# Rotated q and k through DRAM in two transfers, and more raw weight pieces fetched at the start

## The chip, the cores and the metric

The kernel runs on one core of a Trainium2 chip. A core has five engines with a queue of instructions each, run in order: TensorE (PE in the profile; its weight loads are shown apart as PEld), VectorE (DVE), ScalarE (ACT), GpSimd (POOL) and SyncE (SP). SP computes nothing here; it starts DMA transfers. The engines wait for each other through semaphores. The metric is the time of one execution on the device in microseconds (us). The kernel before takes 928.59 us, the median of three runs.

## The reference

The first half is a gated linear recurrence with complex decays, for 4 batches x 8 heads, 768 time steps and heads of 48. The second half is a feed-forward with RMS norm and SwiGLU on the 3072 resulting rows of 384. Cut to its core:

```python
mag = np.sqrt(a_re * a_re + a_im * a_im)
scale = np.minimum(mag, 0.999) / (mag + 1e-06)
a_re_n, a_im_n = (a_re * scale, a_im * scale)
for t in range(S):
    ar, ai = (a_re_n[:, :, t, :, None], a_im_n[:, :, t, :, None])
    new_re = ar * S_re - ai * S_im
    new_im = ar * S_im + ai * S_re
    kv = np.einsum('bhd,bhe->bhde', k[:, :, t], v[:, :, t])
    S_re, S_im = (new_re + kv, new_im)
    y[:, :, t] = np.einsum('bhd,bhde->bhe', q[:, :, t], S_re)
...
rms = np.sqrt(np.mean(x * x, axis=-1, keepdims=True) + 1e-06)
xn = x / rms * rms_g
g = xn @ w_gate
silu = g * (1.0 / (1.0 + np.exp(-g)))
val = xn @ w_val
return (silu * val @ w_out).astype(np.float32)
```

The weights of the feed-forward arrive as 64-bit floats, 384 x 1536 twice and 1536 x 384 once.

## The kernel before

The time steps are cut into chunks of 128 (`C`), six to a batch, 24 in all (`N`). Two chunks are a unit (12 units), three chunks are a group (8 groups). Everything is computed in 32-bit floats.

**Gates, a unit at a time** (`gates(u)`). `load_gates(u)` (L514) fetches the decays `re`, `im` and `q`, `k` of a unit, each as a tile of 128 partitions x 3 x 256. DVE and ACT work out, along the time axis, the running product `p` of the magnitudes (a scan, L579), its last value per chunk (`ends`, L582), and the running phase. q is multiplied by the magnitude and k by its inverse. Then both are multiplied by cosine and sine of the phase (L607 to L610), which gives four tiles `k`, `ks`, `q`, `qs`. In these tiles the features lie on 128 partitions in three blocks.

**The copies.** TensorE needs them otherwise: 96 partitions (48 cosine rows, 48 sine rows), and the eight heads side by side. L619 does this by DMA from SBUF to SBUF. For each chunk and each of q and k there are two parts of three blocks, 12 transfers of 64 KB. L625 moves the decays of a chunk, six transfers of half a KB. L629 loads `v` of the chunk. All are issued by SP.

**Chunks.** `scores(n)` multiplies k and q of every head (L705), DVE masks the product (L707), and PE transposes k (L716). `finish(n)` adds the chunk to the state (L728, multiplied by the decay on DVE), makes y from the masked scores and from the state (L739, L741), norms it (L745 to L751) and transposes it to `xT` (L758, L759).

**Feed-forward, a group at a time** (`feed_forward(g)`). For each of 12 blocks of 128 columns PE makes the gate and the value (L776), ACT the SiLU (L779), DVE the product `hT`. Then PE makes the three output chunks with `wo` (L787), ACT copies them out of PSUM (L792), SP stores them (L794).

**Weights.** `load_weights` yields 18 pieces of 768 KB: six for `wg` and six for `wv` in turns, then six for `wo`. `narrow` fetches one (L656) into one of two buffers `raw` and turns it into 32-bit floats by one instruction on ACT (L662) and six on DVE (lines L663 to L671 through the helpers L501 and L504, and directly at L665 and L669). The first group's feed-forward asks for two pieces every second block and for the six of `wo` after its last block.

**Order.** The program is written as generators: `run` steps the work of chunk n, and between its steps work of the last group's feed-forward (`filler`) and of the next unit's gates (`ahead`). A planner then lays out each engine's queue when the kernel is built. It takes an instruction when it reckons its operands and buffers ready, and prefers the one written earlier, so that later work moves forward into gaps. From then on each queue's order is fixed, DMA issues among it. The lines that the change touches are those of `load_gates`, the end of `gates`, `narrow` and `load_weights`, the decay in `finish` (L730), the weight calls in `feed_forward`, and the main loop.

Of the kernel before, what the change touches and what calls it, by code (L numbers as in the profile page):

```python
# [28 lines left out]
P = 128  # L29
# [442 lines left out]
def fast(tc, ctx, qT, kT, v, a_re, a_im, w_gate, w_val, w_out, rms_g, out, H, bad):  # L472
# [23 lines left out]
    ffn = ctx.enter_context(tc.tile_pool(name="ffn", bufs=2))  # L496
# [12 lines left out]


    UN = [dict() for _ in range(NU)]

    def load_gates(u):
# [14 lines left out]

    first_loads = load_gates(0)

    zeros = consts.tile([P, T], FP32, name="zeros")
    nc.gpsimd.memset(zeros, 0.0)
# [9 lines left out]
    nc.gpsimd.memset(mid, -(RE_MAX + RE_MIN) / 2)  # L542
    width = consts.tile([P, 1], FP32, name="width")
    nc.gpsimd.memset(width, -(RE_MAX - RE_MIN) / 2)
    ends = consts.tile([P, NU, ND, UC], FP32, name="ends")
    range_ = consts.tile([P, NU], FP32, name="range_")

    def gates(u):
# [1 line left out]
        re, im, q, k = (t[x] for x in ("re", "im", "q", "k"))  # L550
        act_ = nc.scalar.activation

        s, w, y, r, p, ks, qs = (prep.tile([P, ND, T], FP32, tag=x, name=x)
                                 for x in ("s", "w", "y", "r", "p", "ks", "qs"))
        act_(out=s, in_=re, func=AF.Square)
        act_(out=w, in_=im, func=AF.Square)
        tt(s, s, w, ALU.add)
# [18 lines left out]
        wc = w.rearrange("p j (c t) -> p j c t", t=C)  # L576
# [27 lines left out]
        act_(out=s, in_=im, func=AF.Sin, scale=2 * PI)  # L604
        act_(out=y, in_=w, func=AF.Sin, scale=-2 * PI, bias=halfpi)
        yield
        tt(ks, k, s)  # L607
        tt(k, k, y)
        tt(qs, q, s)
        tt(q, q, y)  # L610
        rot = {"kc": k, "ks": ks, "qc": q, "qs": qs}
        yield
        for i in range(UC):
            n = u * UC + i
            for name in ("k", "q"):
                to = U[n][name] = unit.tile([D2, H, C], FP32, tag=name, name=name, bufs=3)
                for a, part in enumerate("cs"):
                    for j in range(ND):
                        nc.sync.dma_start(  # L619
                            out=to[a * D + j * L:a * D + (j + 1) * L],  # L620
                            in_=rot[name + part][:, j, i * C:(i + 1) * C])
            de = U[n]["decay"] = unit.tile([D2, H], FP32, tag="decay", name="decay", bufs=5)
            for a in range(2):
                for j in range(ND):
                    nc.sync.dma_start(  # L625
                        out=de[a * D + j * L:a * D + (j + 1) * L],
                        in_=ends[:, u, j, i:i + 1])
            U[n]["v"] = unit.tile([C, H, D], FP32, tag="v", name="v", bufs=3)
            nc.sync.dma_start(out=U[n]["v"].rearrange("t h d -> t (h d)"),  # L629
                              in_=v[n * C:(n + 1) * C, :])  # L630
        yield


# [13 lines left out]


    FW = 2 * P

    def narrow(stage, to, src):

        rows, cols = to.shape[1:]
        n = rows * cols
        raw = stage.tile([P, rows, 2 * cols], I32, tag="raw", name="raw", bufs=2)
        nc.sync.dma_start(out=raw, in_=src)  # L656
# [8 lines left out]
        nc.vector.tensor_scalar(out=t, in0=g, scalar1=3, scalar2=0x3FFFFFFF,  # L665
                                op0=ALU.logical_shift_left, op1=ALU.bitwise_and)
# [6 lines left out]
    def load_weights(stage):  # L673

        for f in range(0, DF, FW):
            for to, ap in ((wg, w_gate), (wv, w_val)):
                to = to[:, :, f:f + FW]
                if ap.dtype == FP32:
                    nc.sync.dma_start(out=to, in_=ap.rearrange("(c p) f -> p c f", p=P)[:, :, f:f + FW])
                else:  # L680
                    narrow(stage, to, ap.bitcast(I32).rearrange("(c p) f -> p c f", p=P)
                           [:, :, 2 * f:2 * (f + FW)])
                yield
        for c in range(0, NF, 2):
            to, ap = wo[:, c:c + 2], w_out
            if ap.dtype == FP32:
                nc.sync.dma_start(out=to, in_=ap.rearrange("(c p) f -> p c f", p=P)[:, c:c + 2])
            else:
                narrow(stage, to, ap.bitcast(I32).rearrange("(c p) f -> p c f", p=P)[:, c:c + 2])
            yield  # L690


    U = [dict() for _ in range(N)]
    G = [dict() for _ in range(NG)]

    def scores(n):
# [23 lines left out]
    def finish(n):  # L720
# [4 lines left out]
        if n % NCH < NCH - 1:  # L725
            ps = ps_a.tile([D2, H, D], FP32, tag="a", name="state_ps")
            for h in range(H):
                nc.tensor.matmul(ps[:, h], lhsT=u["kt"][:, h], rhs=vv[:, h], start=True, stop=True)  # L728
            new = unit.tile([D2, H, D], FP32, tag="state", name="state")
            decay = u["decay"].unsqueeze(2).to_broadcast([D2, H, D])  # L730
# [30 lines left out]
        yield  # L761


    def feed_forward(g, pieces):
        xT = G[g]["xT"]
        hT = ffn.tile([P, NF, GT], FP32, tag="hT", name="hT", bufs=1)
        for f in range(NF):
            fs = slice(f * P, (f + 1) * P)
            if f * P % FW == 0:
                next(pieces, None)  # L770
                next(pieces, None)
            gp = ps_g.tile([P, GT], FP32, tag="g", name="gate_ps")
            vp = ps_g.tile([P, GT], FP32, tag="g", name="val_ps")
            for p_, w_ in ((gp, wg), (vp, wv)):
                for d in range(ND):
                    nc.tensor.matmul(p_, lhsT=w_[:, d, fs], rhs=xT[:, d], start=d == 0,  # L776
                                     stop=d == ND - 1)
# [35 lines left out]
    for n in range(N + 1):  # L813
# [13 lines left out]
        if n % GC == 0 and n:  # L827
            for _ in filler:
                pass
            filler = feed_forward(n // GC - 1, pieces)  # L830

    ne = NU * ND * UC
    ok = act.tile([P, 2 * ne + NU], FP32, tag="ok", name="ok", bufs=1)
# [63 lines left out]
```

## Time and profile before

The profiled execution is a separate one; its own time stands beside the span, which runs from its first to its last instruction.

| | us |
|---|---|
| three runs | 928.59, 923.82, 930.76 |
| the profiled execution | 935.99 |
| its span | 934.3 |
| PE busy | 798.5 (85%) |
| PEld busy | 544.1 (58%) |
| DVE busy | 430.5 (46%) |
| ACT busy | 370.7 (40%) |
| POOL busy | 17.1 (2%) |
| first matmul starts at | 43.57 |

In the rows of the profile, L705 is line 705 of the kernel, and `out<-in` names tiles. "x16" is a count. In a row of the groups, the numbers behind the first bar are the busy time in all and the mean of one instruction in ns. What stands behind the second bar is idle time of that engine just before. In a timeline the first two numbers are start and duration, and a bracket at the end tells how long the engine had been idle and what released it. In a DMA row the numbers are KB of one transfer and the median time from issue to landing. In a row of waits they are the total, the count and the longest. The granted clock of TensorE is given as a share of its full speed; its mean over the execution was 0.916.

### The profile page before, as it was taken

Reading aid. Unit: us, or ns where it says so; the run is one execution under the profiler, and the core shown is the slowest. Engines: PE = TensorE matmul, PEld = TensorE weight load, DVE = VectorE, ACT = ScalarE, POOL = GpSimd, SP = SyncE. Lnnn points to the kernel's source line nnn. Section 1 sums busy time; section 2 is a strip of 40 time slices with the busy share of each in tenths; the row PEclk is TensorE's granted clock in tenths of the full one; section 3 lists DMA queues with packets and bytes.
Section 4 is the critical chain, followed back from the end, with each engine's and each line's share of the span. In section 5 each row is a group of like instructions: output and inputs, shape, how many; then the busy total and the mean of one; then the engine's idle time right before and its main releaser. Section 6 shows DMA issues by size and latency. Waiting matters only on the chain.

```text
span 934.3 us, 9261 instructions
## 1 busy us (share of the span) xinstructions
PE 798.5 (85%) x3370; PEld 544.1 (58%) x3370; DVE 430.5 (46%) x641; ACT 370.7 (40%) x530; POOL 17.1 (2%) x41
## 2 busy tenths in 40 slices
PE   0134885388688899999999999999999999999997
PEld 0133865245446557667666767676667666765554
DVE  5896454797797364362554622735612101110110
ACT  5756354552653282461657613727411111110110
POOL 0000000000000000000000000000000000000000
PEclk9998575688797999898999999999999999899999
DMA  7422333147344232232023222221211010000000
GB/s 227 104 81 69 87 93 102 40 111 201 88 118 107 76 99 58 69 93 60 21 66 94 77 59 77 60 59 24 63 26 43 8 43 1 1 1 26 1 1 29
DMA packets 105574, 62.14 MB, mean 67 GB/s; under 512 B 28720, under 2 KB 99376, under 8 KB 105520
## 3 DMA queue, kind: packets, MB, share of 16 engines
q1 hardware_dynamic: 105520, 61.46, 24.1%
q8 instruction: 29, 0.48, 0.2%
q14 instruction: 25, 0.20, 0.1%
HBM read 37.75 MB, written 4.72 MB: 45 GB/s over the span
## 4 chain that ended last, share of the span: by engine, by line
PE 76%; DVE 10%; ACT 3%; issue 2%; DMA 1%; POOL 0%; DVEq 0%; ACTq 0%; SPq 0%
PE out_ps L787 20%; PE gate_ps L776 20%; PE val_ps L776 18%; PE y_ps L739 5%; PE y_ps L741 4%; PE s_ps L705 3%; PE state_ps L728 3%; PE kt_ps L716 1%; PE xT_ps L758 1%; DVE t L504 1%; DVE g L504 1%; DVE w L504 1%; DVE im L504 1%; DVE p L579 1%; DMA raw<-in_w_gate_dram 1%
## 5 line engine op out<-in xcount | busy, mean ns | idle before, releaser
L776 PE MATMUL val_ps<-xT,wv 128*128 128x384 f32 x576 | 210.4, 503 | 24.8 <-DVE wv L501 24.2
L776 PE MATMUL gate_ps<-xT,wg 128*128 128x384 f32 x576 | 217.0, 516 | 2.3 <-DVE wg L501 1.7
L787 PE MATMUL out_ps<-wo,hT 128*128 128x384 f32 x576 | 200.9, 507 | 8.5 <-DVE wo L501 7.2
L776 PEld LDWEIGHTS val_ps<-xT,wv 128*128 128x128 f32 x576 | 113.0, 197 | 106.6 <-DVE wv L501 26.3
L787 PEld LDWEIGHTS out_ps<-wo,hT 128*128 128x128 f32 x576 | 112.4, 199 | 85.2 <-issue 9.3
L776 PEld LDWEIGHTS gate_ps<-xT,wg 128*128 128x128 f32 x576 | 112.6, 202 | 75.1 <-issue 12.3
L501 DVE TENSOR_TENSOR hT<-val_ps,sg 128x384 f32<-128x384 f32 x96 | 53.3, 555 | 219.0 <-PE val_ps L776 194.5
L779 ACT ACTIVATE sg<-gate_ps 128x384 f32<-128x384 f32 x96 | 47.1, 490 | 180.2 <-PE gate_ps L776 177.0
L705 PE MATMUL s_ps<-q,k 96*128 96x128 f32 x384 | 55.5, 305 | 56.5 <-DMA k<-k 43.6
L705 PEld LDWEIGHTS s_ps<-q,k 96*128 96x128 f32 x384 | 54.6, 220 | 62.5 <-issue 44.0
L739 PE MATMUL y_ps<-v,am 128*128 128x48 f32 x384 | 78.9, 303 | 0.0
L741 PE MATMUL y_ps<-state,q 96*128 96x48 f32 x320 | 70.5, 306 | 0.0
L739 PEld LDWEIGHTS y_ps<-v,am 128*128 128x128 f32 x384 | 65.6, 221 | 0.8
L792 ACT COPY ot<-out_ps 128x384 f32<-128x384 f32 x24 | 11.4, 477 | 118.1 <-PE out_ps L787 112.1
L741 PEld LDWEIGHTS y_ps<-state,q 96*128 96x128 f32 x320 | 57.1, 222 | 0.0
L745 ACT ACTIVATE x<-y_ps 128x384 f32<-128x384 f32 x24 | 11.8, 491 | 107.5 <-PE y_ps L741 98.6
L728 PE MATMUL state_ps<-v,kt 128*96 128x48 f32 x320 | 34.9, 269 | 22.8 <-DVE am L707 22.8
L728 PEld LDWEIGHTS state_ps<-v,kt 128*96 128x96 f32 x320 | 34.6, 187 | 27.5 <-DVE am L707 23.7
L707 DVE TENSOR_TENSOR am<-s_ps,causal 128x512 f32<-128x512 f32 x48 | 32.5, 687 | 39.2 <-PE s_ps L705 39.1
L746 DVE TENSOR_SCALAR ssq<-ssq 128x1 f32<-128x1 f32 x24 | 3.7, 153 | 71.9 <-ACT x L745 71.9
L717 ACT COPY kt<-kt_ps 128x384 f32<-128x384 f32 x40 | 17.3, 478 | 46.6 <-PE kt_ps L716 46.6
L779 ACT ACT_TABLE_LOAD x27 | 34.6, 1283 | 0.5
(97 smaller groups left out, 714.3 us busy)
## 6 DMA issues: line engine op xcount, KB each, us to landing
re<-in_a_re_dram SPq DMA_DIRECT2D x36, 128.0 KB, 2.8
im<-in_a_im_dram SPq DMA_DIRECT2D x36, 128.0 KB, 2.8
q<-in_q_dram SPq DMA_DIRECT2D x24, 192.0 KB, 3.1
k<-in_k_dram SPq DMA_DIRECT2D x24, 192.0 KB, 3.7
v<-in_v_dram SPq DMA_DIRECT2D x24, 192.0 KB, 2.8
raw<-in_w_gate_dram SPq DMA_DIRECT2D x6, 768.0 KB, 5.6
raw<-in_w_val_dram SPq DMA_DIRECT2D x6, 768.0 KB, 5.2
q<-qs SPq DMA_DIRECT2D x72, 64.0 KB, 2.4
```

Source lines behind the costliest of these rows:

```text
L501: nc.vector.tensor_tensor(out=o, in0=x, in1=y, op=op)
L504: nc.vector.scalar_tensor_tensor(out=o, in0=x, scalar=c, in1=y, op0=op0, op1=op1, **kw)
L705: nc.tensor.matmul(ps[:, h], lhsT=k[:, a * hh + h], rhs=q[:, a * hh + h], start=True, stop=True)
L707: nc.vector.tensor_tensor(out=am[:, a * hh:(a + 1) * hh], in0=ps, op=ALU.mult, in1=causal.unsqueeze(1).to_broadcast([C, hh, C]))
L717: nc.scalar.copy(out=kt[:, a * hh:(a + 1) * hh], in_=ps)
L728: nc.tensor.matmul(ps[:, h], lhsT=u["kt"][:, h], rhs=vv[:, h], start=True, stop=True)
L739: nc.tensor.matmul(ps[:, h], lhsT=am[:, h], rhs=vv[:, h], start=True, stop=prev is None)
L741: nc.tensor.matmul(ps[:, h], lhsT=q[:, h], rhs=prev[:, h], start=False, stop=True)
L745: nc.scalar.activation(out=x, in_=y, func=AF.Square, accum_out=ssq)
L776: nc.tensor.matmul(p_, lhsT=w_[:, d, fs], rhs=xT[:, d], start=d == 0, stop=d == ND - 1)
L779: nc.scalar.activation(out=sg, in_=gp, func=AF.Silu)
L787: nc.tensor.matmul(ps, lhsT=hT[:, f, i * C:(i + 1) * C], rhs=wo[:, f], start=f == 0, stop=f == NF - 1)
```

## The change

The four products of the rotation are written straight into one tile `rot` of 128 x 12 x 2 x 129, with the chunk's decay in column 129 beside both parts of q. One DMA writes a chunk's share of it to a tile in DRAM, and one reads it back in the layout that TensorE needs: 96 partitions, k and q, eight heads, 129 columns. This replaces the 18 transfers of L619 and L625. q and k as loaded have one buffer instead of two, and `v` is fetched with the gates' inputs, into four buffers instead of three.

Raw weight pieces are fetched apart from narrowing them. The first five are asked for before the first gates: three into a pool `early` of three buffers, two into the stage pool as before. From piece 3 on, piece i + 2 is asked for when piece i is to be narrowed. The first three are narrowed, in the program's order, at the end of step n = 3. The pool `early` is closed there and the feed-forward's pool opened in its place; the pieces after them are narrowed as far as a block needs. The first unit's `im` is issued on ACT's queue, and an extra activation at the start makes ACT load its function table. The loads of the second unit are written behind the first unit's gates.

```diff
+    dram = ctx.enter_context(tc.tile_pool(name="dram", bufs=2, space=DRAM))
...
+            queue = nc.scalar if u == 0 and name == "im" else nc.sync
             for j in range(ND):
-                nc.sync.dma_start(out=t[name][:, j], in_=rows[j][:, :, c * C:c * C + T])
-        for name, ap in (("q", qT), ("k", kT)):
-            t[name] = prep.tile([P, ND, T], FP32, tag=name, name=name, bufs=2)
+                queue.dma_start(out=t[name][:, j], in_=rows[j][:, :, c * C:c * C + T])
+        for name, ap in (("k", kT), ("q", qT)):
+            t[name] = prep.tile([P, ND, T], FP32, tag=name, name=name)
...
+        for n in range(u * UC, (u + 1) * UC):
+            U[n]["v"] = unit.tile([C, H, D], FP32, tag="v", name="v", bufs=4)
+            nc.sync.dma_start(out=U[n]["v"].rearrange("t h d -> t (h d)"),
+                              in_=v[n * C:(n + 1) * C, :])
...
+    rot = consts.tile([P, 4 * ND, UC, C + 1], FP32, name="rot")
+    nc.vector.memset(rot[:, :, :, C:], 0.0)
...
+    nc.scalar.activation(out=width, in_=width, func=AF.Abs_reciprocal_sqrt)
+    nc.gpsimd.memset(width, -(RE_MAX - RE_MIN) / 2)
...
+        nc.vector.tensor_copy(
+            out=rot[:, 2 * ND:, :, C].rearrange("p (a j) c -> p a j c", j=ND),
+            in_=ends[:, u].unsqueeze(1).to_broadcast([P, 2, ND, UC]))
...
-        tt(ks, k, s)
-        tt(k, k, y)
-        tt(qs, q, s)
-        tt(q, q, y)
-        rot = {"kc": k, "ks": ks, "qc": q, "qs": qs}
+        for i, (x, f) in enumerate(((k, y), (k, s), (q, y), (q, s))):
+            tt(rot[:, i * ND:(i + 1) * ND, :, 0:C], by_chunk(x), by_chunk(f))
...
-            for name in ("k", "q"):
-                to = U[n][name] = unit.tile([D2, H, C], FP32, tag=name, name=name, bufs=3)
-                for a, part in enumerate("cs"):
-                    for j in range(ND):
-                        nc.sync.dma_start(
-                            out=to[a * D + j * L:a * D + (j + 1) * L],
-                            in_=rot[name + part][:, j, i * C:(i + 1) * C])
-            de = U[n]["decay"] = unit.tile([D2, H], FP32, tag="decay", name="decay", bufs=5)
...
+            way = dram.tile([4 * DM, C + 1], FP32, tag="way", name="way")
+            nc.sync.dma_start(out=way.rearrange("(r p) t -> p r t", p=P), in_=rot[:, :, i])
+            to = unit.tile([D2, 2, H, C + 1], FP32, tag="kq", name="kq", bufs=3)
+            nc.sync.dma_start(out=to.rearrange("d x h t -> d x (h t)"),
+                              in_=way.rearrange("(x d h) t -> d x (h t)", x=2, h=H))
+            U[n]["k"], U[n]["q"] = to[:, 0, :, 0:C], to[:, 1, :, 0:C]
+            U[n]["decay"] = to[:, 1, :, C:]
...
-    def narrow(stage, to, src):
+    narrowed = [0]
+    EARLY = 3
+
+    def fetch(pool, to, src):
+        raw = pool.tile([P, to.shape[1], 2 * to.shape[2]], I32, tag="raw", name="raw")
+        nc.sync.dma_start(out=raw, in_=src)
+        return raw
+
+    def narrow(stage, to, raw):
...
+        for i in range(EARLY + 2):
+            get(i)
+        yield
+        for i, (to, ap, c, f) in enumerate(parts):
+            if i >= EARLY and i + 2 < len(parts):
+                get(i + 2)
+            if i in raws:
+                narrow(stage, to, raws.pop(i))
+            narrowed[0] += 1
+            yield
...
-                next(pieces, None)
-                next(pieces, None)
+                while narrowed[0] < 2 * (f * P // FW + 1):
+                    next(pieces)
...
-    pieces = load_weights(stage)
-    load_gates(1)
+    first = ExitStack()
+    pieces = load_weights(first.enter_context(tc.tile_pool(name="early", bufs=EARLY)), stage)
+    next(pieces)
     for _ in gates(0):
         pass
+    load_gates(1)
...
+            if n == GC:
+                for _ in range(EARLY):
+                    next(pieces)
+                first.close()
+                ffn = ctx.enter_context(tc.tile_pool(name="ffn", bufs=2))
```

The tile `ok` of the final range check now shares a buffer with `x` of the chunks.

More of the change, by code (lines that the diff above doesn't have):

```diff
@@ L511, in fast @@
     UN = [dict() for _ in range(NU)]
+    U = [dict() for _ in range(N)]
     def load_gates(u):
@@ L551, in gates @@
         act_ = nc.scalar.activation
-        s, w, y, r, p, ks, qs = (prep.tile([P, ND, T], FP32, tag=x, name=x)
-                                 for x in ("s", "w", "y", "r", "p", "ks", "qs"))
+        s, w, y, r, p = (prep.tile([P, ND, T], FP32, tag=x, name=x)
+                         for x in ("s", "w", "y", "r", "p"))
         act_(out=s, in_=re, func=AF.Square)
@@ L574, in gates @@
         stt(w, w, EPS_MAG, r, ALU.subtract, ALU.min)
[L576 removed]
+        by_chunk = lambda x: x.rearrange("p j (c t) -> p j c t", t=C)
+        wc = by_chunk(w)
         nc.vector.tensor_copy(out=starts[:, :, :, 0:1], in_=wc[:, :, :, 0:1])
@@ L614, in gates @@
             n = u * UC + i
-            for name in ("k", "q"):
-                to = U[n][name] = unit.tile([D2, H, C], FP32, tag=name, name=name, bufs=3)
-                for a, part in enumerate("cs"):
-                    for j in range(ND):
-                        nc.sync.dma_start(
-                            out=to[a * D + j * L:a * D + (j + 1) * L],
-                            in_=rot[name + part][:, j, i * C:(i + 1) * C])
-            de = U[n]["decay"] = unit.tile([D2, H], FP32, tag="decay", name="decay", bufs=5)
[L623 to L630, printed above, removed]
+            way = dram.tile([4 * DM, C + 1], FP32, tag="way", name="way")
[5 more added lines that the diff above has]
+            U[n]["decay"] = to[:, 1, :, C:]
         yield
@@ L649, in fast @@
     FW = 2 * P
-    def narrow(stage, to, src):
+    narrowed = [0]
[5 more added lines that the diff above has]
+    def narrow(stage, to, raw):
         rows, cols = to.shape[1:]
         n = rows * cols
-        raw = stage.tile([P, rows, 2 * cols], I32, tag="raw", name="raw", bufs=2)
-        nc.sync.dma_start(out=raw, in_=src)
         words = raw.rearrange("p c f -> p (c f)").rearrange("p (n two) -> p n two", two=2)
@@ L671, in narrow, with load_weights, get @@
         tt(to, as_to(t.bitcast(FP32)), to, ALU.add)
-    def load_weights(stage):
+    def load_weights(early, stage):
+        parts = []
         for f in range(0, DF, FW):
[L676 to L685, printed above, removed]
+            parts += [(to[:, :, f:f + FW], ap, slice(0, ND), f) for to, ap in ((wg, w_gate), (wv, w_val))]
+        parts += [(wo[:, c:c + 2], w_out, slice(c, c + 2), 0) for c in range(0, NF, 2)]
+        raws = {}
+        def get(i):
+            to, ap, c, f = parts[i]
             if ap.dtype == FP32:
-                nc.sync.dma_start(out=to, in_=ap.rearrange("(c p) f -> p c f", p=P)[:, c:c + 2])
+                nc.sync.dma_start(out=to, in_=ap.rearrange("(c p) f -> p c f", p=P)[:, c, f:f + to.shape[2]])
             else:
-                narrow(stage, to, ap.bitcast(I32).rearrange("(c p) f -> p c f", p=P)[:, c:c + 2])
+                raws[i] = fetch(early if i < EARLY else stage, to, ap.bitcast(I32)
+                                .rearrange("(c p) f -> p c f", p=P)[:, c, 2 * f:2 * (f + to.shape[2])])
+        for i in range(EARLY + 2):
[7 more added lines that the diff above has]
+            narrowed[0] += 1
             yield
-    U = [dict() for _ in range(N)]
     G = [dict() for _ in range(NG)]
@@ L729, in finish @@
             new = unit.tile([D2, H, D], FP32, tag="state", name="state")
-            decay = u["decay"].unsqueeze(2).to_broadcast([D2, H, D])
+            decay = u["decay"].to_broadcast([D2, H, D])
             if prev is None:
@@ L761, in finish, with feed_forward @@
         yield
-    def feed_forward(g, pieces):
+    def feed_forward(g, pieces, ffn):
         xT = G[g]["xT"]
@@ L829, in fast @@
                 pass
-            filler = feed_forward(n // GC - 1, pieces)
+            if n == GC:
[3 more added lines that the diff above has]
+                ffn = ctx.enter_context(tc.tile_pool(name="ffn", bufs=2))
+            filler = feed_forward(n // GC - 1, pieces, ffn)
     ne = NU * ND * UC
-    ok = act.tile([P, 2 * ne + NU], FP32, tag="ok", name="ok", bufs=1)
+    ok = act.tile([P, DM], FP32, tag="x", name="ok", bufs=1)[:, 0:2 * ne + NU]
     for to, in_, limit, op in ((ok[:, 0:ne], ends.rearrange("p u j c -> p (u j c)"), P_MIN, ALU.is_ge),
```

3 lines of the change are left out of this document (1 added, 2 removed).

## The prediction

> **What bounds the kernel now.** I read, in this order: the page's busy shares and slices, the stages by windows, the queue of SyncE in order of time, the waits, the groups by line, and the DMA rows. First the page: the span, and the busy share of TensorE (PE) in 40 equal slices.
>
> ```profile
> span 934.3 us, 9261 instructions
> PE   0134885388688899999999999999999999999997
> ```
>
> From the fifteenth slice on (327 us, and by the windows below from 311 us) PE is busy without a gap; before that it isn't. The windows give the stages, with VectorE (DVE) and ScalarE (ACT) beside it (columns: PE, PEld, DVE, ACT, POOL, clock, DMA share, GB/s):
>
> ```profile
> core 0: us, PE busy (x) PEld busy (x) DVE busy (x) ACT busy (x) POOL busy (x), PEclk, DMA share, GB/s
> 0.00:12.00 12.00, 0.00 (x0) 0.00 (x0) 1.77 (x2) 6.78 (x8) 2.27 (x17) 1.00 0.66 179
> 12.00:60.00 48.00, 5.04 (x24) 4.77 (x24) 44.13 (x61) 30.93 (x37) 0.00 (x0) 1.00 0.52 148
> 60.00:176.00 116.00, 75.49 (x381) 68.13 (x381) 63.64 (x92) 58.68 (x82) 2.75 (x5) 0.70 0.28 76
> 176.00:311.00 135.00, 100.67 (x382) 63.91 (x383) 114.35 (x161) 59.41 (x80) 2.45 (x3) 0.83 0.42 113
> 311.00:905.00 594.00, 594.00 (x2513) 393.89 (x2512) 206.04 (x326) 213.45 (x323) 9.61 (x16) 0.97 0.17 47
> ```
>
> So the time has two parts. From 311 us PE sets the end, at 594.00 busy of 594.00, and nothing off PE can shorten that part. Before 311 us PE waits for things that DVE makes: the gates of each pair of chunks, and the weights, which DVE narrows from 64-bit words in 18 pieces. The second part of the feed-forward of the first three chunks needs the last piece, so the ramp ends when piece 18 is narrowed. When DVE works on pieces is shown by its instructions that read a raw piece, two for each piece:
>
> ```profile
> 0.00:60.00 60.00, 5.71 (x6) 2.70 (x3) 1.00 0.55 154
> 60.00:176.00 116.00, 0.00 (x0) 0.76 (x1) 0.70 0.28 76
> 176.00:311.00 135.00, 28.57 (x30) 12.79 (x15) 0.83 0.42 113
> ```
>
> Three pieces before 60 us, none from 60 to 176 us, fifteen after. In the middle window DVE had 116 - 63.64 = 52.4 us free and used none of it for weights. The queue of SyncE (SP, which issues every DMA) says why:
>
> ```profile
> 32.11 0.54 SPq L656 DMA_DIRECT2D raw<-in_w_gate_dram  x1
> ...
> 38.96 0.96 DVE L504 SCALAR_TENSOR_TENSOR wv<-raw,g 128x768 f32<-128x768 uint32 x1
> ...
> 65.85 1.91 SPq L619 DMA_DIRECT2D k<-k  x3
> ...
> 73.58 3.80 SPq L625 DMA_DIRECT2D decay<-ends  x6
> ...
> 140.84 0.49 SPq L656 DMA_DIRECT2D raw<-in_w_val_dram  x1
> 141.37 0.49 SPq L656 DMA_DIRECT2D raw<-in_w_gate_dram  x1
> ```
>
> Piece 2 (counting from 0) is fetched at 32 us. The buffer for piece 3 is free at 38.96 + 0.96 = 39.9 us, when DVE has last read piece 1. Yet piece 3 is fetched at 140.84 us, behind the copies of rotated q and k (L619) and decays (L625) of three units. The queue runs in order, and it also stands still for the results that it copies. PE then stands for the late weights (waits of SP from 30 to 315 us, and of PE up to 315 us):
>
> ```profile
> SPq L619 <- DVE k L501: 46.9, 4, 21.3
> SPq L656 <- DVE wv L504: 33.3, 5, 16.8
> PE val_ps L776 <- DVE wv L501: 24.2, 4, 12.0
> PE out_ps L787 <- DVE wo L501: 7.2, 3, 3.3
> ```
>
> **The change, part by part.** *The copies.* Per unit of two chunks L619 and L625 issue 2 x (12 + 6) = 36 DMAs; three take 1.91 us and six 3.80 us, so 0.63 us each and 36 x 0.63 = 22.7 us of SP. Afterwards there are 2 x 2 = 4, about 2.5 us. Over 12 units SP loses some 240 us of issuing. None of it is on PE's path after 311 us. Before that it is what stands ahead of the pieces.
>
> *The pieces.* Five are fetched before the first gates instead of two, three into buffers of their own. Every later one is asked for as soon as a stage buffer is free, with 4 DMAs of rotations ahead of it per unit instead of 36. So DVE can use its free time between 60 and 176 us. How much? It won't reach 100%, since it waits in order for PE and ACT. The rate with pieces at hand is in the windows: 44.13/48 = 92% from 12 to 60 us, 114.35/135 = 85% from 176 to 311 us. I take 85%, the window with the same mixture of feed-forward and gates. From 60 to 176 us DVE then does 0.85 x 116 = 98.6 us, 35.0 us more than now. That is seven pieces at the price of one:
>
> ```profile
> L504 DVE SCALAR_TENSOR_TENSOR g<-wg,raw 128x768 f32<-128x768 f32 x6 | 5.7, 949 | 0.0
> L504 DVE SCALAR_TENSOR_TENSOR t<-g,t 128x768 int32<-128x768 int32 x18 | 17.1, 952 | 0.2
> L665 DVE TENSOR_SCALAR t<-g 128x768 int32<-128x768 int32 x18 | 9.9, 551 | 0.1
> ```
>
> The third form comes twice in a piece (L665, L669) and the first two stand for four passes: 4 x 0.95 + 2 x 0.55 = 4.9 us. What is left for the last window is 114.35 - 35.0 = 79.4 us, at 85% 93.7 us: the ramp ends at 176 + 93.7 = 269.7 instead of 311 us, **-41 us**. PE has room for this: it was busy for 181 us up to 311 us, at a low clock, some 141 us at full clock (5 + 75.49 x 0.70 + 100.67 x 0.83), and from 44 to 270 us there are 226. Ends: nothing gained (0), and DVE full from 60 us on, where the idle 52.4 + (135 - 114.35) = 73 us all go (-73).
>
> *The way through DRAM.* Rotated q, k and decays of a chunk are written (4 x 384 rows of 516 bytes, 792 KB) and read back, and the read waits on SP for the write. The nearest rows:
>
> ```profile
> k<-in_k_dram SPq DMA_DIRECT2D x24, 192.0 KB, 3.7
> raw<-in_w_gate_dram SPq DMA_DIRECT2D x6, 768.0 KB, 5.6
> k<-ks SPq DMA_DIRECT2D x72, 64.0 KB, 2.5
> out_dram<-ot SPq DMA_DIRECT2D x24, 192.0 KB, 1.9
> 34.06 0.95 DVE L501 TENSOR_TENSOR k<-k,y 128x768 f32<-128x768 f32 x1
> 43.57 3.76 PE L705 MATMUL s_ps<-q,k 96*128 96x128 f32 x16 [43.57 <-DMA k<-k]
> 60.76 0.68 DVE L707 TENSOR_TENSOR am<-s_ps,causal 128x512 f32<-128x512 f32 x1
> 62.83 0.94 DVE L501 TENSOR_TENSOR k<-k,r 128x768 f32<-128x768 f32 x1
> ```
>
> The read has long rows: 5.6 us as a raw piece of the same size. The write has short rows: between 5.6 us and four of the 512-byte loads one after another, 4.1 x 3.7 = 15.2 us; I take 7 us, nearer to the raw piece, as a store of 192 KB lands in 1.9 us. The first chunk's way is then 12.6 us against 43.57 - 35.01 = 8.6 now: **+4 us** in unit 0. It may be less, since DVE reaches the scores late: it masks the first at 60.76 us though PE had them at 47.3 us, a cover of 13 us. As DVE's order is made anew I don't count on that cover for unit 0, but do for the later ones, where the ramp has other work; without it the price is 4 us a unit, with some five units in the ramp. While SP stands for a write, the raw fetches and loads behind it wait up to 7 us, twice a unit, which two raw buffers cover.
>
> The Trainium skill says, in "DMA: Bandwidth & Descriptors", section "Issuing engines are not separate DMA queues", that the time to start a DMA is usually small beside the DMA itself. By that rule fewer DMAs would be worth next to nothing and the sum would be the second rival's. The trace has 0.63 us of issue beside a landing of 2.5 us for the small copies, but 36 issues in a row, so the rule does not hold for a queue that runs in order.
>
> *The start.* im goes out on ACT's queue and the table of functions is loaded before the data come.
>
> ```profile
> 4.94 1.28 ACT L555 ACT_TABLE_LOAD   x1 [4.94 <-DMA re<-in_a_re_dram]
> 7.28 0.84 ACT L556 ACTIVATE w<-im 128x768 f32<-128x768 f32 x1 [0.20 <-DMA im<-in_a_im_dram]
> 8.14 1.28 ACT L558 ACT_TABLE_LOAD   x1
> ```
>
> One load of 1.28 us, perhaps both, leaves ACT's path: **-2 us** (0 to -2.6).
>
> *The rest, at nothing.* The new copy of the decays into rot is one small DVE instruction a unit: under 0.55 us, the shortest pass above, so under 3 us in the ramp and 0 after it. k and q in one buffer each: the next unit's loads wait for the rotations, done at 35 us for unit 0, while unit 1's k is first scaled at 62.83 us; a load of 3.7 us fits, and would cost 3.7 us a unit if not. The feed-forward's buffers take the memory of the three early pieces; DVE has read those before 60 us already now, and hT is first written when three chunks are through. PE reads k and q from rows of 516 bytes. No row shows such a pitch; the nearest are two forms that read am and q in blocks of 512 bytes:
>
> ```profile
> L739 PE MATMUL y_ps<-v,am 128*128 128x48 f32 x384 | 78.9, 303 | 0.0
> L741 PE MATMUL y_ps<-state,q 96*128 96x48 f32 x320 | 70.5, 306 | 0.0
> ```
>
> They differ by 3 ns with 128 and 96 rows, which says little of an odd pitch. I take zero; 384 + 160 + 320 = 864 matmuls read k or q, and 45 ns on each would eat the whole gain.
>
> *Sum.* -41 + 4 - 2 = -39 us. The profiled run took 935.99 us, 1.7 us beyond its span, and so would give 897. It lies 7.4 us above the median of 928.59, from which the same difference gives **890 us**.
>
> **The rivals.** *Second: DVE's free time can't be filled.* The waits of DVE from 44 to 315 us speak for it:
>
> ```profile
> DVE ssq L746 <- ACT x L745: 27.6, 8, 6.4
> DVE xT L759 <- PE xT_ps L758: 13.7, 6, 4.6
> DVE hT L501 <- PE val_ps L776: 10.7, 4, 4.4
> ```
>
> Together 52.0 us, in which DVE stands at the head of its order for PE and could not narrow anything, unless pieces are placed ahead of the waiting instruction. If pieces only move and the waits stay, the gain is the start and at most two pieces (2 x 4.9 us) less the 4 us: 0 to -8 us, 920 to 929. Against it: with pieces at hand DVE ran at 92% and 85%.
>
> *Third, slower: the round trip paces the chunks.* If the write takes 15.2 us, the second chunk of a unit arrives 2 x 15.2 + 5.6 = 36 us after the rotation, against 8.6 + 12 x 0.63 = 16.2 now. That is 20 us more; less the cover of 13 us it is 7 us a unit, 35 us over the five or so units of the ramp, and SP stands meanwhile, so the pieces gain nothing: about 964 us. It decides from a round trip of 8.6 + 13 = 21.6 us. Against it: a store of 192 KB lands in 1.9 us, sooner than loads of that size.
>
> *Fourth: more than forecast.* With the pieces ahead, DVE needs fewer gates done before the ramp ends, and PE's clock (0.70 and 0.83 in the ramp) rises as its gaps close: up to the end of -73 us, some 855.
>
> **How the numbers follow.** The forecast (gain 15 to 60 us, 868 to 914) gets 0.68, the fourth 0.12, the second 0.12, the third 0.08. About 1% (9 us) is what a measurement can tell here. Faster by more is the forecast with the fourth, 0.80; within is the second, 0.12; slower 0.08. The range reaches from the end at -75 us, 853, to within the second rival, 925.
>
> **What would show it.** Right: pieces read by DVE between 60 and 176 us (some 14 raw-reading instructions there, now 0); DVE at about 85% in that window; PE without gaps from about 270 us; the waits of PE for wv and wo together under 10 us; SP with 4 long DMAs a unit, the write landing in about 7 us. Wrong: PE waiting for the read of k and q again and again in the ramp; DVE's idle time under ssq, xT and hT as long as now; s_ps, kt_ps or y_ps matmuls longer in the stage after the ramp; a raw fetch again 50 us or more after its buffer came free.

## The result, and the profile after

| | before | changed |
|---|---|---|
| median of 4 runs, us | 929.61 | 888.31 |
| range, us | 923.82 to 930.76 | 884.13 to 890.75 |
| the profiled execution, us | 935.99 | 884.13 |
| its span, us | 934.3 | 882.3 |
| PE busy in it, us | 798.5 | 773.3 |
| span less PE busy, us | 135.8 | 109.0 |

The changed kernel takes 0.9563 of the time before, 95% interval 0.9507 to 0.9619, a gain of 40.6 us; 890 was predicted. The two profiled spans differ by 52.0 us, but the profiled execution of before lies 6.4 us above its median and that of the changed kernel 4.2 us below, which is 10.6 of these. Among the kernels below, some executions are slower than the others of the same kernel; the ratios leave these out, the medians do not, and the profiles of `early_only` and `way_twice` show such executions, so sizes read from these two are only rough.

The page of the changed kernel first: span, PE's total, and PE's slices.

```profile
span 882.3 us, 8797 instructions
PE 773.3 (88%) x3370; PEld 530.1 (60%) x3370; DVE 426.8 (48%) x654; ACT 356.2 (40%) x520; POOL 23.2 (3%) x42
PE   0051879888879999999999999999999999999997
```

PE is full from the thirteenth slice on, not the fifteenth. Then its windows, with the same columns as before, and the instructions of DVE that read a raw piece (DVE, ACT, clock, DMA share, GB/s):

```profile
60.00:176.00 116.00, 80.53 (x406) 65.06 (x404) 92.29 (x138) 68.14 (x92) 6.13 (x5) 0.74 0.64 154
60.00:271.00 211.00, 156.90 (x719) 118.56 (x718) 167.18 (x247) 111.41 (x152) 8.61 (x8) 0.77 0.58 146
271.00:882.30 611.30, 605.18 (x2587) 400.35 (x2586) 214.69 (x345) 206.32 (x322) 12.20 (x16) 0.99 0.26 63
```

```profile
60.00:176.00 116.00, 12.61 (x14) 4.54 (x5) 0.74 0.64 154
176.00:311.00 135.00, 16.83 (x18) 7.29 (x8) 0.87 0.50 130
```

Fourteen raw-reading instructions stand where there were none. The last piece is narrowed at 271 us, and PE's last gap of the ramp ends half a microsecond before (DVE, then PE, in order of time):

```profile
270.14 0.94 DVE L501 TENSOR_TENSOR wo<-t,wo 128x768 f32<-128x768 f32 x1
```

```profile
270.56 0.55 PE L774 MATMUL xT_ps<-ident,xn 128*128 128x128 f32 x3 [1.46 <-ACT xn L767]
```

What is left at 271 us is what was left before at 311 us. The same window of the kernel before is

```profile
311.00:934.30 623.30, 617.30 (x2584) 407.29 (x2582) 206.60 (x327) 214.89 (x326) 9.61 (x16) 0.97 0.17 46
```

2584 matmuls there, 2587 here. So 40 us of the difference between the spans are the ramp. Of these, 26.9 us are idle time of PE (129.8 us up to 311 us before, 102.9 us up to 271 us now), and 13.1 us are its busy time (181.2 and 168.1 us, for 787 and 785 matmuls). The mean granted clock of the two stretches is 0.81 and 0.82, so the clock's mean does not account for the 13.1 us; where they come from stays open. The other 12 us lie in the stage without gaps, at a clock of 0.97 against 0.99, and 10.6 us is how far the two executions lie from their medians. The waits of PE up to 315 us, those of before that the prediction did not show and then those of after:

```profile
PE s_ps L705 <- DMA k<-k: 43.6, 1, 43.6
PE state_ps L728 <- DVE am L707: 22.8, 4, 12.5
PE xT_ps L758 <- ACT xn L751: 15.0, 6, 3.4
PE s_ps L705 <- DVE am L707: 12.9, 1, 12.9
```

```profile
PE s_ps L721 <- DMA kq<-way: 77.3, 5, 48.8
PE xT_ps L774 <- ACT xn L767: 15.4, 6, 6.4
PE gate_ps L792 <- DVE wg L501: 4.8, 2, 3.1
```

The waits for `wv` and `wo` (31.4 us) and for the mask `am` (35.7 us) are gone. In their place PE waits for k and q from DRAM, 48.8 us for the first chunk (43.6 before) and 77.3 - 48.8 = 28.5 us in four later units.

### The profile page after: what moved, and what is told of

Same layout as the page of the kernel before. It is cut to its first block, busy times and chain, and to the rows that moved or that the text cites. A ratio compares the mean times of both kernels' runs of the same rounds, so it can differ in the third digit from the quotient of the medians.

```text
span 882.3 us, 8797 instructions
## 1 busy us (share of the span) xinstructions
PE 773.3 (88%) x3370; PEld 530.1 (60%) x3370; DVE 426.8 (48%) x654; ACT 356.2 (40%) x520; POOL 23.2 (3%) x42
## 4 chain that ended last, share of the span: by engine, by line
PE 80%; DMA 10%; DVE 6%; ACT 2%; issue 1%; SPq 1%; POOL 0%; ACTq 0%; DVEq 0%
PE val_ps L792 20%; PE gate_ps L792 20%; PE out_ps L803 19%; PE s_ps L721 6%; PE y_ps L755 5%; DMA way<-rot 4%; PE y_ps L757 4%; DMA kq<-way 4%; PE state_ps L744 3%; PE kt_ps L732 2%; DVE rot L501 1%; PE xT_ps L774 1%; DMA raw<-in_w_gate_dram 1%; DVE p L592 1%; DVE g L504 1%
## 5 line engine op out<-in xcount | busy, mean ns | idle before, releaser
L792 PE MATMUL gate_ps<-xT,wg 128*128 128x384 f32 x576 | 209.4, 501 | 5.5 <-DVE wg L501 4.8
L803 PE MATMUL out_ps<-wo,hT 128*128 128x384 f32 x576 | 192.8, 491 | 0.2
L792 PEld LDWEIGHTS gate_ps<-xT,wg 128*128 128x128 f32 x576 | 109.0, 196 | 73.7 <-issue 7.9
L803 PEld LDWEIGHTS out_ps<-wo,hT 128*128 128x128 f32 x576 | 108.7, 192 | 71.7 <-issue 1.8
L721 PE MATMUL s_ps<-kq 96*128 96x128 f32 x384 | 57.2, 311 | 77.3 <-DMA kq<-way 77.3
L721 PEld LDWEIGHTS s_ps<-kq 96*128 96x128 f32 x384 | 55.5, 224 | 84.0 <-DMA kq<-way 55.6
L755 PE MATMUL y_ps<-v,am 128*128 128x48 f32 x384 | 76.0, 294 | 0.0
L757 PE MATMUL y_ps<-state,kq 96*128 96x48 f32 x320 | 68.2, 298 | 0.0
L757 PEld LDWEIGHTS y_ps<-state,kq 96*128 96x128 f32 x320 | 55.1, 215 | 0.3
L765 POOL TENSOR_TENSOR rs<-ssq,mhalf 128x1 f32<-128x1 f32 x24 | 20.8, 867 | 754.7 <-DVE ssq L762 754.7
```

The source lines that it names most:

```text
L721: nc.tensor.matmul(ps[:, h], lhsT=k[:, a * hh + h], rhs=q[:, a * hh + h], start=True, stop=True)
L755: nc.tensor.matmul(ps[:, h], lhsT=am[:, h], rhs=vv[:, h], start=True, stop=prev is None)
L757: nc.tensor.matmul(ps[:, h], lhsT=q[:, h], rhs=prev[:, h], start=False, stop=True)
L765: nc.gpsimd.tensor_tensor(out=rs, in0=ssq, in1=mhalf, op=ALU.pow)
L803: nc.tensor.matmul(ps, lhsT=hT[:, f, i * C:(i + 1) * C], rhs=wo[:, f], start=f == 0, stop=f == NF - 1)
```

## The experiments

Each edit makes the planner lay all queues out anew, so one kernel's times say less than the agreement of several. The table gives the ratio to the kernel before with its 95% interval, the gain (one less the ratio, times 929.6 us), and from each profile PE's idle time (span less PE busy), the raw-reading instructions of DVE from 60 to 176 us, and the start of the first scores. Idle time and start are left empty for `early_only` and `way_twice`.

| kernel | ratio | gain, us | PE idle, us | raw 60-176 | first scores, us |
|---|---|---|---|---|---|
| changed | 0.9563 (0.9507 to 0.9619) | 40.6 | 109.0 | 14 | 48.79 |
| way_only | 0.9725 (0.9659 to 0.9791) | 25.6 | 120.2 | 12 | 53.22 |
| early_only | 1.008 (0.9988 to 1.0172) | -7.4 | | 3 | |
| raw_on_pool | 0.9552 (0.9506 to 0.9597) | 41.6 | 116.7 | 20 | 49.75 |
| raw_on_act | 0.9544 (0.9470 to 0.9618) | 42.4 | 115.0 | 21 | 54.05 |
| early_pool | 0.9652 (0.9596 to 0.9708) | 32.4 | 117.9 | 22 | 45.2 |
| no_start | 0.9612 (0.9559 to 0.9664) | 36.1 | 117.5 | 11 | 52.68 |
| early0 | 0.9584 (0.9526 to 0.9642) | 38.7 | 112.9 | 13 | 50.42 |
| way_twice | 0.9786 (0.9723 to 0.9849) | 19.9 | | 8 | |
| way_halves | 0.9489 (0.9433 to 0.9544) | 47.5 | 100.5 | 12 | 46.63 |
| later_on_pool | 0.9894 (0.9848 to 0.9940) | 9.9 | 138.1 | 10 | 51.05 |
| pool_start | 0.9497 (0.9440 to 0.9554) | 46.8 | 110.8 | 20 | 43.67 |
| pool_start2 | 0.9599 (0.9537 to 0.9662) | 37.3 | 113.4 | 20 | 42.6 |

**Do the pieces stand behind SP's copies?** The theory of the prediction against one in which DVE cannot use its free time. `way_only` is the kernel before with the copies through DRAM (and q and k as loaded in one buffer each) and nothing else of the change:

```diff
-            for name in ("k", "q"):
...
+            nc.sync.dma_start(out=way.rearrange("(r p) t -> p r t", p=P), in_=rot[:, :, i])
+            to = unit.tile([D2, 2, H, C + 1], FP32, tag="kq", name="kq", bufs=3)
+            nc.sync.dma_start(out=to.rearrange("d x h t -> d x (h t)"),
+                              in_=way.rearrange("(x d h) t -> d x (h t)", x=2, h=H))
```

> The kernel before with one part of the change: rotated q, k and decays go through DRAM in one write and one read a chunk (q and k as loaded in one buffer each); weight pieces, v and the start stay as before. Queue theory (the 36 small copies of a unit in SP's queue hold back the weight pieces, and taking them out is the gain): at least 30 of the 41 us gained, 885 to 900 us, ten or more raw-reading instructions on DVE between 60 and 176 us, where before had none. Buffer rival (the five pieces fetched at the start are the gain): 915 us or more, few or none of those instructions there. Round-trip rival (the way through DRAM costs the ramp more than it gives): above 930 us.

It took 907.03 us, a gain of 25.6 us. The twelve raw-reading instructions are what the queue theory named, but the gain is short of its 30 us and the time lies outside its 885 to 900 us: the theory has the direction here, and not the whole size. `raw_on_pool` leaves the copies alone and takes the pieces out of their queue, by one word:

```diff
-        nc.sync.dma_start(out=raw, in_=src)
+        nc.gpsimd.dma_start(out=raw, in_=src)
```

> The kernel before, with one word changed: weight pieces are fetched through GpSimd's queue instead of SP's; copies, buffers and all else as before. Queue theory: pieces no longer stand behind the copies, so DVE narrows between 60 and 176 us and at least 30 us are gained without any way through DRAM, 880 to 900 us. If the copies themselves (their number, landing or traffic) are what costs: no gain, 920 us or more.

It took 888.6 us: the gain of the whole change without any part of it. In POOL's queue, in order of time, each of these four pieces goes out within 0.6 us of DVE's last read of the buffer that it takes:

```profile
35.01 0.76 POOL L656 DMA_DIRECT2D raw<-in_w_gate_dram  x1 [30.40 <-DVE wg L504]
48.02 0.76 POOL L656 DMA_DIRECT2D raw<-in_w_val_dram  x1 [12.26 <-DVE wv L504]
61.52 0.76 POOL L656 DMA_DIRECT2D raw<-in_w_gate_dram  x1 [12.74 <-ACT r L585]
71.17 0.76 POOL L656 DMA_DIRECT2D raw<-in_w_val_dram  x1 [8.89 <-DVE wv L504]
```

Before, the fetches of 35, 48 and 61 us stood at 32.11, 140.84 and 141.37 us. `raw_on_act` makes the same word `scalar`.

> The kernel before with one word changed: raw pieces fetched on ACT's queue. If what costs is only that a piece stands behind SP's copies: 880 to 900 us, as on POOL. If a queue that waits for its own work holds the pieces as much, ACT's being ahead of its operands more often than POOL's: 900 to 930 us.

890.05 us, the same. So it is leaving SP's queue that counts, not POOL. `early_only` is the changed kernel with the small copies back (the `way` lines above reversed, and q, k in two buffers):

> The changed kernel with the copies undone: rotated q, k and decays are copied by 36 small DMAs a unit as before; five weight pieces at the start, v early, im on ACT's queue and the early function table stay. Queue theory: piece 5 is again fetched behind the copies of three units, so the ramp gains only what two more pieces are worth and the start, 5 to 15 us: 913 to 925 us. Buffer rival: nearly the whole gain, 885 to 900 us.

No gain: 944.78 us, where the queue theory had expected 5 to 15 us; why not even that came stays open. SP's queue fetches the sixth piece at 188 us, behind the copies, however many pieces were fetched at the start:

```profile
188.07 0.34 SPq L532 DMA_DIRECT2D v<-in_v_dram  x1
188.45 0.43 SPq L663 DMA_DIRECT2D raw<-in_w_val_dram  x1
188.93 0.49 SPq L663 DMA_DIRECT2D raw<-in_w_gate_dram  x1
189.51 2.04 SPq L630 DMA_DIRECT2D k<-k  x3
```

`early_pool` is this kernel with the pieces behind the first five on POOL's queue:

```diff
-        nc.sync.dma_start(out=raw, in_=src)
+        queue.dma_start(out=raw, in_=src)
...
+                                nc.sync if i < EARLY + 2 else nc.gpsimd)
```

> The changed kernel without the way through DRAM (the 18 small copies and the loads of q and k in two buffers as before), and with the raw pieces behind the first five fetched on POOL's queue. With the pieces on SP this kernel took 944.8 us, with the pieces on POOL in the changed kernel it was 922.3. If SP's queue is the cause and the copies as such cost nothing: 865 to 895 us, as for the kernel before with its pieces on POOL (888.6), and PE's waits for k in the ramp under 10 us beyond the first chunk (28.5 in the changed kernel). If asking for a piece only when another is to be narrowed puts it behind POOL's waits for ssq, as in the changed kernel with pieces on POOL: 905 to 930 us, with 10 or fewer raw-reading instructions of DVE from 60 to 176 us.

895.93 us, just beyond the first theory's range and outside the second's; 22 raw-reading instructions against 3, and PE's waits for k and q beyond the first chunk are 11.6 us, just over the 10 expected. Moving 13 issues to another queue is worth 39.8 us here. In all five kernels pieces that do not stand behind SP's small copies are narrowed between 60 and 176 us and pieces behind them are not, and DVE could use its free time; the sizes were missed in `way_only` and `early_only`. That `way_only` gains 25.6 us where leaving the queue gains 41.6 leaves a question: what does the way through DRAM cost? (Of the 11.2 us of PE's idle time that `way_only` has more than the changed kernel, 9.7 are waits for k and q: 87.0 against 77.3 us.)

**Is the round trip on PE's path after unit 0?** The prediction said hidden. `way_twice` copies each chunk once more, from DRAM to DRAM, between write and read:

```diff
+            way2 = dram.tile([4 * DM, C + 1], FP32, tag="way2", name="way2")
+            nc.sync.dma_start(out=way2, in_=way)
...
-                              in_=way.rearrange("(x d h) t -> d x (h t)", x=2, h=H))
+                              in_=way2.rearrange("(x d h) t -> d x (h t)", x=2, h=H))
```

> The changed kernel with one more transfer of the same size between the write and the read, from DRAM to DRAM, on SP's queue. It makes the round trip longer by about 6 to 9 us for each chunk. If the round trip is on PE's path only in unit 0 and hidden in the later units of the ramp, as predicted: 894 to 900 us. If PE waits for it in every unit of the ramp, as its waits for k and q show (five waits, 48.8 us with the first chunk, 28.5 us without): five units by 9 to 18 us for two chunks, 905 to 960 us. PE's waits for k and q then grow by more than 30 us in all; by the first theory by less than 15.

By the ratios it is (0.9786 - 0.9563) x 929.6 = 20.7 us slower than the changed kernel. The added transfer lands in 6.5 us; paid once it would be some 6.5 us, so by this estimate it is paid about three times. PE's wait in its profile points the same way:

```profile
PE s_ps L723 <- DMA kq<-way: 108.6, 5, 57.4
```

Beyond the first chunk 51.2 us, where the changed kernel waits 28.5. The 22.7 us more lie between the two theories, which had under 15 and over 30; the time is in the range of the second. The extra transfer also holds SP's queue longer (8 raw-reading instructions instead of 14), so not all of the 20.7 us need be the path's. `way_halves` goes the other way, with k and q written and read apart:

```diff
...
+            half = way.rearrange("(x r p) t -> x p r t", x=2, p=P)
+            back = way.rearrange("(x d h) t -> x d (h t)", x=2, h=H)
+            for x in range(2):
+                nc.sync.dma_start(out=half[x], in_=rot[:, 2 * ND * x:2 * ND * (x + 1), i])
+            for x in range(2):
+                nc.sync.dma_start(out=to[:, x].rearrange("d h t -> d (h t)"), in_=back[x])
```

> The changed kernel with k and q of a chunk written and read apart: two writes and two reads of half the size, both writes ahead of both reads. The read of k waits for its own write only, so that the round trip is shorter by some 2 to 4 us, for two more issues of some 1.2 us for each chunk. If the round trip is on the path in each unit of the ramp: a gain of 3 to 12 us, 876 to 885 us. If it is hidden behind unit 0, or if the transfers' fixed cost is most of it: 886 to 895 us.

882.92 us, in the range of the first theory, and PE's waits shrink to 15.4 us beyond the first chunk:

```profile
PE s_ps L724 <- DMA kq<-way: 62.0, 3, 46.6
```

Its interval overlaps that of the changed kernel, so the gain of 7 us is not shown by the times alone; the waits, in both directions, do show that PE stands for the round trip. It does so mostly in the second unit: of the changed kernel's 28.5 us 17.28 are there, and 1.89, 3.14 and 6.21 in the next three.

**What else carries the rest?** `early0` fetches two pieces at the start instead of five (`EARLY = 0`), `no_start` takes the first `im` back to SP's queue and drops the extra activation.

> The changed kernel (888.3 us) with two raw pieces fetched ahead in place of five. Before with the way through DRAM alone took 907.0 us, and the start was worth about 4 us, which leaves some 15 us of the gain without an owner. If the three early buffers own it, now that SP's queue is short: 898 to 906 us, and about 10 raw-reading instructions of DVE from 60 to 176 us where the changed kernel has 14. If they are worth nothing, as they were beside the small copies: at most 892 us, with 13 or 14 such instructions.

893.3 us by the median, 1.3 above the range named; by the ratio within the interval of the changed kernel, with 13 raw-reading instructions. The three buffers are worth nothing that can be measured.

> The changed kernel with im of the first unit back on SP's queue and without the activation that loads ACT's table early. Prediction: 2 us of the gain go (0 to 2.6), 888 to 891 us, the same within what can be measured. Rival, that the start is worth much more as it shifts everything behind it: 5 us or more lost.

892.21 us: 4.5 us of the gain, between the two expectations and again within the intervals. The 15 us between `way_only` and the changed kernel have thus no single owner: 1.9 and 4.5 us, neither resolved, and the rest, such as the order of the loads, was not tried by itself.

**Does SP's standing for writes hold pieces up?** `later_on_pool` is the changed kernel with the later 13 pieces on POOL's queue.

> The changed kernel with the first five raw pieces fetched on SP's queue as now and the other 13 on POOL's. SP stands 55.9 us for writes of rotations before 315 us, and raw pieces wait behind it. If that standing still costs: a gain of 5 to 20 us, 868 to 883 us, and 17 or more raw-reading instructions of DVE from 60 to 176 us (14 in the changed kernel). If DVE has all the pieces that it can use: 884 to 893 us, with 13 to 15.

922.28 us: much slower than either theory had it. POOL's queue now holds a piece itself, behind a norm that waits for its chunk:

```profile
78.51 0.91 POOL L659 DMA_DIRECT2D raw<-in_w_val_dram  x1 [10.55 <-ACT w L573]
110.89 1.20 POOL L766 TENSOR_TENSOR rs<-ssq,mhalf 128x1 f32<-128x1 f32 x1 [31.47 <-DVE ssq L763]
112.23 0.78 POOL L659 DMA_DIRECT2D raw<-in_w_gate_dram  x1
```

and PE waits 102.5 us for k and q instead of 77.3. Both are in the profile, but why the new order made chunks this late was not told apart. The changed kernel's own queue answers the question for one piece. The buffer of the sixth piece is free at 74.72 + 0.95 = 75.67 us, and SP fetches it at 84.57 us, right behind reads of k and q that wait for their writes and are issued up to 79.92 + 4.55 = 84.47 us:

```profile
74.72 0.95 DVE L504 SCALAR_TENSOR_TENSOR wv<-raw,g 128x768 f32<-128x768 uint32 x1
```

```profile
84.57 0.41 SPq L659 DMA_DIRECT2D raw<-in_w_val_dram  x1
```

So the standing does hold a piece up, by 8.9 us here. (Before, the fourth piece was held for 101 us.) What this costs in time stays open.

**A better version?** `pool_start` is `raw_on_pool` with the first `im` on ACT's queue and the early function table. `pool_start2` is that with the first two pieces left on SP's queue.

> The kernel before with all raw pieces on POOL's queue, the first im on ACT's queue and the early function table. If the start is worth what it was worth in the changed kernel (some 4 us): 882 to 887 us. If the two pieces fetched at 2.8 us hold the first loads up all the same: 886 to 892 us.

> The kernel before with its first two raw pieces on SP's queue as before, the other 16 on POOL's, the first im on ACT's queue and the early function table. If the two pieces fetched at 2.8 us by POOL delay the first chunk (DVE did nothing in the first 12 us, scores at 49.75 instead of 43.57 us): scores at 41 to 44 us and 878 to 884 us, 5 to 10 us below all pieces on POOL (888.6). If the ramp's end is set by the narrowing alone: 885 to 892 us.

883.15 and 890.34 us. The first scores start at 43.67 and 42.6 us as expected of the start. Only the first median is below that of `raw_on_pool` (888.6 us), and the intervals of all three overlap, so that the start is worth something here is not shown. `pool_start` and `way_halves` (883.15 and 882.92 us) have the lowest medians; both overlap the changed kernel's interval, so no version is shown to beat it.

## Why the prediction came out right, and which steps did not

**Right: what held the pieces.** "Behind the copies of rotated q and k" was the cause, shown by taking away the copies (`way_only`, for 25.6 of the 40.6 us) and by taking the pieces out of the queue (`raw_on_pool`, `raw_on_act`, `early_pool`). These signs came as named: 14 raw-reading instructions, PE's waits for `wv` and `wo` gone, and the last piece narrow at 271.1 us (270.14 + 0.94) where 269.7 was forecast. The second rival is refuted by the same count, and DVE's waits under `ssq`, `xT` and `hT` for ACT and `val_ps` fell from 52.0 to 28.1 us. The fourth, some 855 us, did not come.

The page "DMA: Bandwidth & Descriptors" of the Trainium skill, section "Issuing engines are not separate DMA queues", says that initiating DMAs on several engines "will only save the time on the sequencer". The runs differ: the 18 fetches of `raw_on_pool` take 0.7 to 0.9 us each to issue there, yet moving them gained 41.6 us, because what they waited behind moved out of their way.

**Wrong, and cancelling: DVE at 85% and its amount of work.** From 60 to 176 us DVE was busy 92.29 of 116 us, 80%, and from 60 to 271 us 167.18 of 211 us, 79%. The forecast had 98.6 + 79.4 = 178.0 us of work to do there. At 79% that would have ended at 60 + 178.0 / 0.792 = 285 us. But DVE had done 10.8 us less when the last piece was narrow, and 10.8 / 0.792 = 13.6 us brings the end back to 271. That the two errors cancel is luck. By the groups of DVE, what had not run yet is four passes and three scans of the sixth unit's gates, some 6 us, and four masks of 0.69 us; the rest of the 10.8 us is not traced to groups. One of these passes, up to 311 us before and up to 271 us after:

```profile
L501 DVE TENSOR_TENSOR k<-k,r 128x768 f32<-128x768 f32 x6 | 5.7, 951 | 0.1
```

```profile
L501 DVE TENSOR_TENSOR k<-k,r 128x768 f32<-128x768 f32 x5 | 4.7, 949 | 0.0
```

The fourth rival named the gates, and the forecast left them out.

**Failed: "hidden in later units".** The cover of 13 us was DVE reaching the scores late. In the changed kernel that order is gone, and PE waits for k and q again and again in the ramp, which the prediction had named as a sign of being wrong. DVE now waits for the scores, 19.9 us where it was 0.5 (its waits from 44 to 315 us, then the second unit from rotation to scores on DVE, SP and PE):

```profile
DVE am L723 <- PE s_ps L721: 19.9, 10, 3.6
```

```profile
69.59 0.95 DVE L501 TENSOR_TENSOR rot<-q,s 128x768 f32<-128x768 f32 x1
```

```profile
71.51 3.13 SPq L629 DMA_DIRECT2D way<-rot  x2
79.92 4.55 SPq L631 DMA_DIRECT2D kq<-way  x2
```

```profile
86.02 3.75 PE L721 MATMUL s_ps<-kq 96*128 96x128 f32 x16 [17.28 <-DMA kq<-way]
```

The rotation ends at 70.54 us, the scores start at 86.02, and PE had been idle for 17.28 us. This is the third rival's mechanism. It did not decide, because the round trip was 14.1 us in the first unit and 15.5 us in the second, under the 21.6 us from which that rival was to win, and because PE's waits for the mask and the weights that went (35.7 + 31.4 us) outweigh those that came (28.5 us, and 5.2 us more for the first chunk).

**Mis-sized: the way in unit 0 and the start.** The write lands in 8.9 us where 7 was taken, the read in 5.7 as taken:

```profile
way<-rot SPq DMA_DIRECT2D x24, 774.0 KB, 8.9
kq<-way SPq DMA_DIRECT2D x24, 774.0 KB, 5.7
```

In unit 0 the rotation ends at 34.70 us and the scores start at 48.79: 14.1 us against 12.6 forecast, **+5.5** and not +4. The start was to bring the rotation 2 us forward; it ended 0.3 us earlier (35.01 before). In `no_start` it ends at 38.10 us, so the start gives 3.4 us and something else in the change takes 3.1. It is not the copies, since in `way_only` the rotation ends at 34.85 us. The forecast had nothing for that. A suspect is the five pieces of 768 KB fetched beside the first loads, but `early0`, which fetches two there and keeps the start, ends its rotation at 34.86 us, no earlier. Whether the pieces count when `im` is on SP's queue, or the other order of the loads does, no run tells apart.

**Right: the odd pitch at nothing.** In the stage without gaps, from 311 us before and from 271 us now, the matmuls that read k or q take no longer:

```profile
L705 PE MATMUL s_ps<-q,k 96*128 96x128 f32 x240 | 29.2, 275 | 0.0
L741 PE MATMUL y_ps<-state,q 96*128 96x48 f32 x224 | 45.7, 287 | 0.0
```

```profile
L721 PE MATMUL s_ps<-kq 96*128 96x128 f32 x240 | 29.4, 274 | 0.0
L757 PE MATMUL y_ps<-state,kq 96*128 96x48 f32 x224 | 44.0, 279 | 0.0
```

The transposes of k take 246 ns in both.

**The measure itself.** The prediction let the ramp end when the last piece is narrow. That moment predicted this time well, yet it is no measure of the time, and the match is in part luck. In the changed kernel no wait of PE hangs on a piece of `wo`: what ended its last gap at 270.56 us was `xn`. And 13.1 of the 40 us are PE's busy time, for which the sum had no term. In `raw_on_pool` the last piece is narrow at 230.7 us, 40 us before the changed kernel's, and both take 888 us. DVE narrowed ahead of the masks, and PE paid there instead (22.8 us before):

```profile
PE state_ps L728 <- DVE am L707: 41.6, 4, 14.2
```

PE's idle time in the whole span (135.8, 109.0 and 116.7 us) places the kernels better than the ramp's end does, with PE's busy time beside it, which in the stage without gaps moved with the granted clock (617.30 us at 0.97, 605.18 us at 0.99).

## What to carry to other kernels

When an engine with free time is starved, look at what stands ahead of its loads in the issuing queue before making the loads larger or earlier: here one word, another queue for the weights, was worth as much as the whole change. The new queue can hold the loads itself: with 13 pieces on POOL's queue the changed kernel lost 31 us, and POOL's queue held a piece behind a wait of 31.47 us there, though whether that was the cause was not told apart. A cover that comes from the order of another engine is not safe to count on when that order is laid out anew.

## What the runs showed of the hardware

In the changed kernel a write from SBUF to DRAM in rows of 516 bytes took longer to land than the read of the same 774 KB in rows of 4128 bytes (8.9 against 5.7 us; 10.9 against 5.7 in `way_only`). In `way_halves` the halves of 387 KB, issued two in a row, took 7.1 and 4.4 us. The granted clock in the stage where PE has no gaps was 0.97 in one profiled execution and 0.99 in the other, 12 us over the same matmuls, which is more than the two smaller parts of this change that were taken out one at a time (1.9 and 4.5 us).
